# The first batch of an attention-and-FFN kernel: other fills, mask products that open banks, conversions and a raw load in other places

## The chip, the cores and the metric

The kernel runs on one core of a Trainium2 chip. The metric is the time of one execution in device microseconds (us); the median of the runs shown is taken. PE is the matrix engine (PEld its weight loads), DVE, ACT and POOL are the vector, scalar and general engines, SP issues most DMAs.

## The reference

Eight batches of 576 tokens go through attention with eight heads of 64, and the result (4608 tokens of 512) through a two-layer FFN with a gate:

```python
scores = scale * np.matmul(q, k.transpose(0, 1, 3, 2))
mask_local = (rel >= 0) & (rel < stride)
mask_strided = (rel >= 0) & (pos[None, :] % stride == pos[:, None] % stride)
...
attn = np.exp(scores)
attn = attn / (np.sum(attn, axis=-1, keepdims=True) + 1e-09)
return np.matmul(attn, v).astype(np.float32)
...
h = x @ w_in
g = np.where(pos, h, np.where(neg, 0.0, (h + beta) ** 2 / (4.0 * beta)))
return (g @ w_out).astype(np.float32)
```

The weights come as 64-bit floats, held as pairs of 32-bit words.

## The kernel before

**Attention** of a batch is cut into four units: units 0 and 1 are the local heads, units 2 and 3 the strided ones. The masks leave few keys for each query, so a unit is a set of small score products. For unit u the steps have letters, and a string of them (`AGENDA`) gives the order by hand: `s` scores on PE (`qk` of the batch, two pairs of heads), `o` a product of zeros that opens the score banks, `i` the mask added in the bank by a product with the identity (`m_loc`, `m_str`, made by POOL), `g` a plain copy out of PSUM on ACT, `m` copy with mask on DVE, `X`/`x` row maxima on DVE, `S`/`a`/`b` maxima subtracted, `e` exponentials on ACT, `q` row sums on DVE, `p` plus epsilon on ACT, `w`/`r` normalising (a reciprocal on DVE, then a product on DVE for `w`, on POOL for `r`), `f` transposes on PE (`tp`), `c`/`d` copies of them on ACT or DVE (`pT`), `v` the values product on PE (`xp`), `h`/`l` the high and low part of the result (`xq_a` on ACT, `xq_b` on DVE) for the first 512 tokens left to `H`/`M` where the digits ask for the other part. `Z` issues fills: products of zeros into banks that a later step uses, whose result nobody reads.

**Weights** are converted on the chip, block by block (f = 0 to 15, i = 0 for `w_in`, 1 for `w_out`): a raw load of 512 KB (`load_w`, SP queue), then the steps `A`, `L` (ACT), `B` (DVE), `C` (POOL), `D` (ACT, high part; `g` the same on DVE), `E` (DVE, low part). Step `E0.0` finishes block 0 of `w_in`, and so on. While the FFN of the first 512 tokens runs, these conversions stand between its steps.

**The FFN's start.** `up(0, f)` is 12 products of 128x512 into one bank (high times high, high times low, low times high, over four blocks `cc` of channels, of which 0 and 1 are local heads and 2 and 3 strided ones). Blocks f = 0 and 1 are split: `U0`, `V0` are the first 4 products each (high weights, `cc` 0 and 1), `U1`, `V1` the other 8. After them come `1F0`, `1F1` (loads of batch 1's values), `1s0` (scores of batch 1) and `W7` (raw loads of block 7), then `up(0, 2)`, `down(0)`, `1s1`, `up(0, 3)` and so on. `gate(f)` is two passes on ACT and one on DVE, `rounded(f)` two on DVE; `down(f)` waits for them.

**What sets the order.** Each engine runs its instructions in the order in which the code records them, which is the agenda's; a line of the agenda begins with the time at which it is due against the FFN's steps (minus 66.69: all of it ahead of the FFN). The loads of SP are recorded ahead of the agenda: `qk` of batch 0 (four loads), the raw load of block 0, values and raw loads in turn. The first raw load is held back by a copy of one element into its buffer (L447) that reads `qk` 1, so that the load waits for that copy.

Of the kernel before, what the change touches and what calls it, by code (L numbers as in the profile page):

```python
# [1382 lines left out]
```

## Time and profile before

| what | value |
|---|---|
| median of 3 runs | 802.41 us (801.7 to 802.97) |
| the profiled execution's own time | 803.35 us |
| its span in the trace | 801.2 us |
| PE, DVE, ACT, POOL busy | 99%, 77%, 63%, 32% of the span |

The span is what the trace shows from the first instruction to the last; 2.15 us of the profiled execution lie around it. PE's busy time counts every matmul, those of zeros too, and the ends of matmuls are modelled, so 99% doesn't say that the work is at PE's peak; it says that little of the span has no matmul on PE.

### The profile page before, as it was taken

Reading aid. Unit: us, or ns where it says so; the run is one execution under the profiler, and the core shown is the slowest. Engines: PE = TensorE matmul, PEld = TensorE weight load, DVE = VectorE, ACT = ScalarE, POOL = GpSimd, SP = SyncE. Lnnn points to the kernel's source line nnn. Section 1 sums busy time; section 2 is a strip of 40 time slices with the busy share of each in tenths; the row PEclk is TensorE's granted clock in tenths of the full one; section 3 lists DMA queues with packets and bytes.
Section 4 is the critical chain, followed back from the end, with each engine's and each line's share of the span. In section 5 each row is a group of like instructions: output and inputs, shape, how many; then the busy total and the mean of one; then the engine's idle time right before and its main releaser. Section 6 shows DMA issues by size and latency. Waiting matters only on the chain.

```text
span 801.2 us, 17214 instructions
## 1 busy us (share of the span) xinstructions
PE 791.7 (99%) x6641; PEld 646.5 (81%) x6641; DVE 618.7 (77%) x855; ACT 503.6 (63%) x854; POOL 259.6 (32%) x202
## 2 busy tenths in 40 slices
PE   8999999999999999999999999999999999999998
PEld 5778888878888888878888888888888888888886
DVE  4899979898989999978679786675786854566673
ACT  4899764566764555677665455778544667775442
POOL 4466325897674320022141102132424001224000
PEclk9999999999999999999999999999999999999999
DMA  9967878998899999898789778777787676666765
GB/s 345 390 218 250 334 259 291 300 295 301 268 335 315 293 304 349 271 292 272 240 255 305 232 224 262 240 230 225 214 263 238 210 243 195 190 195 188 221 199 167
DMA packets 106224, 208.67 MB, mean 260 GB/s; under 512 B 17696, under 2 KB 30496, under 8 KB 104096
## 3 DMA queue, kind: packets, MB, share of 16 engines
q1 hardware_dynamic: 99088, 178.09, 69.3%
q10 hardware_dynamic: 7056, 29.49, 9.9%
q8 instruction: 53, 0.87, 0.5%
q14 instruction: 27, 0.22, 0.1%
HBM read 160.76 MB, written 46.78 MB: 259 GB/s over the span
## 4 chain that ended last, share of the span: by engine, by line
PE 87%; DVE 4%; DMA 4%; issue 1%; SPq 1%; POOL 1%; ACT 1%; ACTq 0%; DVEq 0%; POOLq 0%
PE yo L1188 22%; PE y L1093 16%; PE zo L1188 11%; PE h L940 9%; PE z L1093 8%; PE xo L1188 5%; PE o L1000 5%; PE x L1093 4%; PE sc L617 3%; PE xp L832 2%; DMA qk<-in_qk_s 1%; DMA v_w<-in_v_w 1%; DMA windows<-t 1%; PE xp L820 1%; DVE st L524 1%
## 5 line engine op out<-in xcount | busy, mean ns | idle before, releaser
L1188 PE MATMUL yo<-hl,wr 128*128 128x512 f32 x768 | 177.6, 390 | 0.0
L1188 PEld LDWEIGHTS yo<-hl,wr 128*128 128x128 f32 x768 | 143.6, 188 | 30.8 <-DVE hl L1050 0.9
L1093 PE MATMUL y<-x,wr 128*128 128x512 f32 x576 | 139.9, 390 | 0.0
L1093 PEld LDWEIGHTS y<-x,wr 128*128 128x128 f32 x576 | 108.0, 188 | 22.5
L940 PE MATMUL h<-xq_a,w 128*128 128x512 f32 x384 | 123.3, 395 | 0.0
L1149 POOL TENSOR_TENSOR ga<-gb,ga 128x1024 f32<-128x1024 f32 x17 | 44.1, 2602 | 235.3 <-DVE ga L950 175.6
L1050 DVE TENSOR_TENSOR hl<-ga,hl 128x1024 fp32r<-128x1024 f32 x48 | 64.1, 1351 | 35.9 <-ACT hl L1049 35.8
L1188 PE MATMUL zo<-hl,wr 128*128 128x512 f32 x384 | 89.3, 391 | 0.0
L940 PEld LDWEIGHTS h<-xq_a,w 128*128 128x128 f32 x384 | 72.0, 188 | 16.3 <-DVE g L950 0.4
L1188 PEld LDWEIGHTS zo<-hl,wr 128*128 128x128 f32 x384 | 71.6, 188 | 15.6 <-DVE hl L1050 0.6
L1049 ACT CAST hl<-ga 128x1024 fp32r<-128x1024 f32 x48 | 49.9, 1050 | 50.9 <-PE yo L1188 16.5
L1093 PE MATMUL z<-x,wr 128*128 128x512 f32 x288 | 73.6, 391 | 0.3 <-DVE ga L1075 0.3
L940 PE MATMUL h<-xq_b,w 128*128 128x512 f32 x192 | 73.6, 391 | 0.1
L1093 PEld LDWEIGHTS z<-x,wr 128*128 128x128 f32 x288 | 53.7, 188 | 12.0 <-DVE ga L1075 0.8
L947 ACT ACTIVATE tmp<-tmp 128x512 f32<-128x512 f32 x96 | 60.8, 633 | 3.1
L1050 DVE TENSOR_TENSOR hl<-gb,hl 128x1024 fp32r<-128x1024 f32 x36 | 49.2, 1379 | 13.8 <-ACT hl L1049 13.7
L516 POOL TENSOR_TENSOR st<-st 128x256 f32<-128x256 f32 x48 | 52.8, 1102 | 15.0 <-DVE st L733 6.2
L1049 ACT CAST hl<-gb 128x1024 fp32r<-128x1024 f32 x36 | 37.7, 1056 | 31.3 <-PE zo L1188 15.3
L950 DVE SCALAR_TENSOR_TENSOR ga<-ga,tmp 128x512 f32<-128x512 f32 x48 | 33.0, 688 | 28.3 <-ACT tmp L947 28.1
L944 ACT ACTIVATE u<-h,half 128x512 f32<-128x512 f32 x48 | 32.9, 686 | 30.1 <-PE h L940 22.5
L481 POOL TENSOR_TENSOR raw<-raw 128x512 uint32<-128x512 uint32 (+1 forms) x33 | 35.4, 1082 | 43.1 <-DVE raw L477 15.5
L710 POOL TENSOR_TENSOR pr<-pr,st 128x384 f32<-128x384 f32 (+3 forms) x18 | 25.7, 1432 | 64.2 <-DVE st L706 64.0
(128 smaller groups left out, 1404.0 us busy)
## 6 DMA issues: line engine op xcount, KB each, us to landing
wr<-ks SPq DMA_DIRECT2D x224, 256.0 KB, 3.9
wr<-kq SPq DMA_DIRECT2D x168, 256.0 KB, 3.4
ks<-st ACTq DMA_DIRECT2D x16, 1024.0 KB, 5.7
raw<-in_w SPq DMA_DIRECT2D x31, 512.0 KB, 7.6
qk<-in_qk_s SPq DMA_DIRECT2D x16, 604.0 KB, 6.5
qk<-in_qk_l SPq DMA_DIRECT2D x16, 576.0 KB, 6.5
kq<-w ACTq DMA_DIRECT2D x16, 512.0 KB, 4.1
out<-kept SPq DMA_DIRECT2D x24, 256.0 KB, 3.8
```

Of the source, the lines that this page charges most:

```text
L481: nc.gpsimd.tensor_tensor(out=raw[:, :, 1], in0=raw[:, :, 1], in1=raw[:, :, 0], op=ALU.add)
L516: eng.tensor_tensor(out=st[:, to, 1], in0=st[:, x, 1], in1=st[:, y, 1], op=op)
L940: nc.tensor.matmul(o_ps[c, f], weight(f, 0, h)[:, x, e:e + P], xq[c][y][:, cc], start=first and n == 0, stop=last and n == len(todo) - 1)
L944: nc.scalar.activation(u, h, AF.Relu, bias=half, scale=0.5)
L947: nc.scalar.activation(u, u, AF.Square)
L950: nc.vector.scalar_tensor_tensor(out=to, in0=h, scalar=1.0, in1=u, op0=ALU.max, op1=ALU.min)
L1000: nc.tensor.matmul(o_ps["o"][d], weight(f, 1, h)[:, x, e:e + P], gs[y], start=f == 0 and n == 0, stop=f == NF - 1 and n == 2)
L1049: nc.scalar.copy(t[:, 0], src)
L1050: nc.vector.tensor_tensor(out=t[:, 1], in0=src, in1=t[:, 0].bitcast(F32), op=ALU.subtract)
L1093: nc.tensor.matmul(to, w_[:, a, c * P:(c + 1) * P], xc[m][:, b, c], start=m in (1, 2, 5) and c + q == 0, stop=c == 1 and q == 2, skip_grou ...
L1149: eng.tensor_tensor(out=to, in0=x, in1=y, op=op)
L1188: nc.tensor.matmul(to, w_[jj][:, a, d * P:(d + 1) * P], t[:, b, jj], start=m in (1, 2, 5) and k + jj + q == 0, stop=k == NP // 2 - 1 and j ...
```

## The change

- **Fills.** The zeros tile becomes a float32 tile (`nothing`), of which `zeros` is a bfloat16 view. `Z` takes a number of products and a letter: without `b` they are float32 (128x384 here), with `b` bfloat16 over the whole bank. Ahead of unit 0's scores stand 2 + 2 of them instead of 17; 1 + 3 + 2 before unit 0's transposes instead of 3 + 14; 2 before the values products of units 0 and 1 each; those before units 2 and 3 are gone.
- **Masks.** For units 1 and 3 the step `I` (new) puts the mask's product first, as the one that opens the bank and closes it; the scores add to it. `o` and `i` of these units are gone (4 products of zeros fewer).
- **First conversion.** `A0.0` stands behind `0e1` on ACT instead of ahead of it.
- **First raw load.** The copy that holds it back reads one element of `m_str` (partition 64) instead of `qk` 1. The raw load of block 2 moves ahead of the values of unit 3.
- **The end of the first batch.** The values of unit 2 come before those of unit 3. `U0`, now 6 products (with low weights), stands between them; `V0`, 6, behind unit 3; then `U1` (4), `U2` (2), `V1`, `V2`. On DVE `E0.0` moves ahead of the low parts of units 2 and 3. `H1`, `M1`, `H2`, `M2` move behind `gate(0)`, which is now in the agenda as `H0`. The steps `A0.1` to `E0.1` are spread forward.
- **Banks.** The transposes and values of the first batch use other banks; from block 4 of the second token chunk on, `up` turns over four banks instead of three.

```diff
--66.69 0Zs0:17 0o0 0s0 0o1 0i0 0X0 0s1 0i1 0S0 0o3 0g1 0x1 0s2 0Zv0:3 0Zf0:3 0m2 0e0 0a1 A0.0 0s3 0i3 0e1 0x2 0q0
--66.69 0p0 0g3 0a2 0q1 0Zf0:9 0e2 0w0 0Zf0:5 0f0 0p1 0x3 0c0 B0.0 0v0 0b3 L0.0 0e3 0r1 0q2 0p2 0f1 C0.0 0r2 0q3
--66.69 A1.0 0d1 D0.0 0p3 0h0 0r3 L1.0 0l0 A2.0 0Zf2:4 0v1 B1.0 0f2 0h1 0d2 0f3 0c3 0Zv3:4 0v3 0l1 0H1 L2.0 C1.0 g1.0 0v2 E1.0
--66.69 0M1 0h3 B2.0 0l3 E0.0 0h2 0H3 C2.0 U0 0l2 g2.0 V0 0M3 U1 0H2 0M2 E2.0 V1 1F0 1F1 A3.0 1s0 A0.1 B3.0 W7
--66.69 B0.1 L0.1
--63.035 A3.1 C0.1 A4.0 A1.1
--59.845 L3.0 C3.0 B1.1 D0.1 L1.1 C1.1 1m0 E0.1 1x0 1a0
+-66.69 0Zs0:2 0Zs0:2b 0o0 0s0 0I1 0i0 0X0 0s1 0S0 0I3 0g1 0x1 0s2 0Zf0:1 0m2 0e0 0a1 0s3 0e1 A0.0 0x2 0q0
+-66.69 0p0 0g3 0a2 0q1 0e2 0w0 0Zf0:3 0Zf0:2b 0f0 0Zv0:2b 0p1 0x3 0c0 B0.0 0v0 0b3 L0.0 0e3 0r1 0q2 0p2 0f1 0Zv1:2b C0.0 0r2 0q3
+-66.69 A1.0 0d1 D0.0 0p3 0h0 0r3 L1.0 0l0 0v1 B1.0 0f2 0h1 A2.0 0d2 0f3 0c3 C1.0 0v2 0l1 g1.0 E0.0 B2.0 0h2
+-66.69 0l2 L2.0 C2.0 A0.1 U0 0v3 0h3 L0.1 E1.0 B0.1 C0.1 0l3 V0 0H3 0M3 g2.0 E2.0 U1 A3.0 U2 V1 V2 B3.0 H0 D0.1 0H1 0M1 E0.1 0H2 0M2 1F0 1F1 1s0 W7
+-63.035 A1.1 A3.1 A4.0
+-59.845 L3.0 C3.0 B1.1 L1.1 C1.1 1m0 1x0 1a0
...
-    zeros = const.tile([P, P], BF16, name="zeros")
-    nc.vector.memset(zeros, 0.0)
+    nothing = const.tile([P, P], F32, name="nothing")
+    nc.vector.memset(nothing, 0.0)
+    zeros = nothing.bitcast(BF16)[:, :P]
...
-            nc.scalar.copy(raws[f][0:1, i, 0:1, 0].bitcast(F32), after)
+            nc.scalar.copy(raws[f][64:65, i, 0:1, 0].bitcast(F32), after)
...
-            N = min(t.shape[1], 256)
+            of = zeros if short_ else nothing
             for _ in range(n):
-                nc.tensor.matmul(t[:, :N], zeros, zeros[:, :1].broadcast_to([P, N]), start=True, stop=True)
+                nc.tensor.matmul(t, of, of[:, :1].broadcast_to(list(t.shape)), start=True, stop=True)
...
+        def masked(u):
+
+            local, b0, _ = UNITS[u]
+            ahead[u, "s"] = ts = banks(u, "s")
+            covered.add(u)
+            done_.add(u)
+            n, W = slots(u)[0], WL if local else WS
+            m = m_loc[:, b0 and 1:][:, :n].unsqueeze(2) if local else m_str.unsqueeze(1).unsqueeze(1)
+            for t in ts:
+                nc.tensor.matmul(t, ident_b, m.broadcast_to([P, n, 2, W]), start=True, stop=True)
...
-            tag = ("b2", "b3") if NF * c + f < NF + 4 else ("b2", "b3", "b0")
+            tag = ("b2", "b3") if NF * c + f < NF + 4 else ("b0", "b1", "b2", "b3")
...
+            kinds_ = (((0, 0), (0, 1), (1, 0)), ((0, 0), (1, 0)), ((0, 1),))[part]
+            todo = [(cc, x, y) for x, y in kinds_ for cc in ((2, 3) if part else (0, 1))]
...
-        load_w(0, 0, loaded[0, 1, "qk"][0:1, 0, 0:1])
+        load_w(0, 0, m_str[64:65, 0:1])
         load_v(0, 0)
         load_v(0, 1)
         load_w(1, 0)
         load_v(0, 2)
+        load_w(2, 0)
         load_v(0, 3)
-        load_w(2, 0)
```

The built programs show the moves. On ACT, from the exponentials of unit 0 on (`pr_0`; `raw` 191 is block 0 of `w_in`, `st_0` unit 0's statistics), before:

```order
L717 ACTIVATE pr_0_297<-pr_0_297 128x768
L469 ACTIVATE raw_191<-raw_191 128x512
L717 ACTIVATE pr_1_333<-pr_1_333 128x384
L725 ACTIVATE st_0_298<-st_0_298 128x12
L676 COPY pr_3_410<-sc_3_0_329 128x4x54
```

and after:

```order
L729 ACTIVATE pr_0_284<-pr_0_284 128x768
L729 ACTIVATE pr_1_318<-pr_1_318 128x384
L470 ACTIVATE raw_191<-raw_191 128x512
L737 ACTIVATE st_0_285<-st_0_285 128x12
L688 COPY pr_3_386<-sc_3_0_314 128x4x54
```

The conversion and unit 1's exponentials have changed places; the small step of unit 0 still stands behind the conversion. On DVE, at the low parts of the last units (`xq_b`) and the low part of the weights (`w_0`; raw 191 is block 0, raw 198 block 1), before:

```order
L903 TENSOR_TENSOR xq_b<-xp_3_0_581,xq_a 128x12x16
L903 TENSOR_TENSOR xq_b<-xp_3_0_581,xq_a 128x2x16
L903 TENSOR_TENSOR xq_b<-xp_3_1_582,xq_a 128x12x16
L903 TENSOR_TENSOR xq_b<-xp_3_1_582,xq_a 128x2x16
L494 TENSOR_TENSOR w_0_516<-raw_191,w_0_516 128x2x256
L903 TENSOR_TENSOR xq_b<-xp_2_0_614,xq_a 128x18x16
L903 TENSOR_TENSOR xq_b<-xp_2_1_615,xq_a 128x18x16
```

and after:

```order
L491 CAST w_0_491<-raw_198 128x2x256
L495 TENSOR_TENSOR w_0_491<-raw_191,w_0_491 128x2x256
L478 TENSOR_SCALAR raw_202<-raw_202 128x512
L915 TENSOR_TENSOR xq_b<-xp_2_0_551,xq_a 128x18x16
L915 TENSOR_TENSOR xq_b<-xp_2_1_552,xq_a 128x18x16
L495 TENSOR_TENSOR w_0_491<-raw_198,w_0_491 128x2x256
L478 TENSOR_SCALAR raw_191<-raw_191 128x512
L915 TENSOR_TENSOR xq_b<-xp_3_0_596,xq_a 128x12x16
```

Block 0's low weights (from raw 191) now come ahead of the low parts of units 2 and 3. On PE, at the last values products and the first products of the FFN, before:

```order
L832 MATMUL xp_2_0_614<-pT_2_568,v_2_None 64x64 x2
L832 MATMUL xp_2_1_615<-pT_2_568,v_2_None 64x64 x2
L940 MATMUL h_0_660<-xq_a,w_0_516 128x512 x2
L940 MATMUL h_0_660<-xq_b,w_0_516 128x512 x2
L940 MATMUL h_1_669<-xq_a,w_0_516 128x512 x2
```

and after:

```order
L844 MATMUL xp_2_0_551<-pT_2_537,v_2_None 64x64 x2
L844 MATMUL xp_2_1_552<-pT_2_537,v_2_None 64x64 x2
L953 MATMUL h_0_589<-xq_a,w_0_491 128x512 x2
L953 MATMUL h_0_589<-xq_b,w_0_491 128x512 x2
L953 MATMUL h_0_589<-xq_a,w_0_491 128x512 x2
L844 MATMUL xp_3_0_596<-pT_3_547,v_3_204 64x64 x2
```

Six products of the FFN's block 0 now stand ahead of unit 3's values, low weights among them.

## Rows read from the trace of the kernel before

**Rows 1.** Stretches: length, busy us (instructions) by engine, PEclk, DMA share, GB/s
```profile
0.00:10.20 10.20, 9.11 (x223) 6.36 (x224) 3.07 (x8) 3.16 (x7) 5.84 (x26) 1.00 0.82 293
10.20:12.55 2.35, 0.00 (x0) 0.00 (x0) 2.06 (x3) 0.20 (x1) 1.61 (x3) 1.00 0.97 356
12.60:16.00 3.40, 3.39 (x49) 2.39 (x49) 1.65 (x3) 1.82 (x7) 0.19 (x1) 0.50 1.03 416
12.55:24.80 12.25, 11.73 (x254) 9.43 (x253) 9.05 (x22) 9.89 (x28) 5.43 (x6) 0.86 1.03 410
25.40:34.00 8.60, 8.46 (x185) 6.48 (x185) 6.66 (x21) 6.83 (x20) 2.08 (x2) 1.00 1.02 407
34.00:100.00 66.00, 65.94 (x550) 53.47 (x551) 63.56 (x119) 60.84 (x112) 36.57 (x34) 1.00 0.77 275
```

**Rows 2.** Timeline of PE: start, length, line, operation, count, [idle before, releaser]
```profile
0.99 3.81 PE L599 MATMUL sc<-zeros 128*128 128x256 bf16 x17 [0.99 <-DVE zeros L379]
...
5.37 1.32 PE L617 MATMUL sc<-qk 64*32 64x64 f32 x96
...
12.61 0.58 PE L599 MATMUL tp<-zeros 128*128 128x256 bf16 x2 [2.51 <-issue]
...
15.11 2.15 PE L599 MATMUL tp<-zeros 128*128 128x256 bf16 x14
17.10 0.82 PE L747 MATMUL tp<-ident,pr 128*128 128x128 f32 x6
...
22.05 1.42 PE L747 MATMUL tp<-ident,pr 128*128 128x128 f32 x11
...
25.44 0.46 PE L832 MATMUL xp<-pT,v 54*64 54x64 f32 x16 [0.78 <-issue]
...
26.53 0.73 PE L940 MATMUL h<-xq_a,w 128*128 128x512 f32 x2
```

**Rows 3.** DMA queue of instructions in 10.2 to 11.3, and 16.0 to 17.3: packets, MB
```profile
q8 instruction: 1, 0.02, 5.1%
...
q8 instruction: 1, 0.02, 4.8%
```

**Rows 4.** Timeline of ACT, columns as for PE
```profile
5.79 0.19 ACT L447 COPY raw<-qk 1x1 f32<-1x1 f32 x1 [3.76 <-DMA qk<-in_qk_l]
...
12.35 0.66 ACT L469 ACTIVATE raw<-raw 128x512 f32<-128x512 f32 x1 [2.31 <-DMA raw<-in_w]
...
13.32 0.20 ACT L725 ACTIVATE st<-st 128x12 f32<-128x12 f32 x1
15.09 1.00 ACT L676 COPY pr<-sc 128x216 f32<-128x216 f32 x4 [1.57 <-PE sc L641]
...
17.63 0.86 ACT L757 COPY pT<-tp 128x384 f32<-128x384 f32 x2 [0.67 <-PE tp L747]
```

**Rows 5.** Timeline of DVE, columns as for PE
```profile
14.17 0.96 DVE L734 TENSOR_TENSOR pr<-pr,st 128x768 f32<-128x768 f32 x1
...
27.62 0.70 DVE L494 TENSOR_TENSOR w<-raw,w 128x512 fp32r<-128x512 f32 x1
28.23 1.31 DVE L903 TENSOR_TENSOR xq_b<-xp,xq_a 128x288 fp32r<-128x288 f32 x2
...
39.52 0.68 DVE L494 TENSOR_TENSOR w<-raw,w 128x512 fp32r<-128x512 f32 x1
```

**Rows 6.** Timelines of POOL (second half of the strided mask) and SP (first raw load)
```profile
6.02 0.54 POOL L398 TENSOR_SCALAR_AFFINE_SELECT m_str<-m_str 64x54 bf16<-64x54 bf16 x2
...
6.00 0.33 SPq L448 DMA_DIRECT2D raw<-in_w  x1
```

**Rows 7.** Line 537, loads of `qk`, to 20 us: first and last issue; issue to landing
```profile
L537 SPq DMA_DIRECT2D qk<-in_qk_l x4: 327/360/417, 0.7 to 18.1; - x4
...
DMA to landing us min/median/max: 3.5/6.3/10.9
```

**Rows 8.** Chain of waits, one piece: start, length, what (the products of `up(0, 2)`)
```profile
33.97 2.96 PE h L940 x12
```

More of the change, by code (lines that the diff above doesn't have):

```diff
@@ L490, in conv_d, with conv_e @@
             copy(to[:, :, 0], whole(raw))
-    def conv_e(f, i):
+    def conv_e(f, i, eng=nc.vector):
         for raw, to in words(f, i):
-            nc.vector.tensor_tensor(out=to[:, :, 1], in0=whole(raw), in1=to[:, :, 0].bitcast(F32), op=ALU.subtract)
+            eng.tensor_tensor(out=to[:, :, 1], in0=whole(raw), in1=to[:, :, 0].bitcast(F32), op=ALU.subtract)
     def blocks(i, j):
@@ L575, in wide @@
             return b > 1 and u == 0
-        probs, flipped, there, ahead, covered = {}, {}, {}, {}, set()
+        probs, flipped, there, ahead, covered, done_ = {}, {}, {}, {}, set(), set()
         def banks(u, kind):
@@ L618, in score @@
                                          qk[:, k0:k0 + W], start=u not in covered,
-                                         stop=u not in covered)
+                                         stop=u not in covered or u in done_, skip_group_check=u in done_)
         def score_0(u):
@@ L909, in in_two @@
             return lambda u: do(u, rest if b == 0 else None)
[L911 removed]
+        steps = {"s": score, "y": score_0, "z": score_1, "m": mask, "o": opened, "I": masked, "i": cover, "g": plain, "X": most_there, "S": below_there, "x": most, "w": norm_v, "a": below_max, "e": expo, "q": total, "p": plus_eps, "k": plus_eps_v, "b": below_max_v, "r": norm,
                  "f": flip, "t": turn, "j": spread, "J": gather, "c": keep, "d": keep_v, "v": value, "V": values_1_3, "h": in_two(high, False), "l": in_two(low, False), "H": in_two(high, True), "M": in_two(low, True),
@@ L916, in go @@
                 if name[0] == "Z":
-                    zero(int(name[2]), name[1], int(name[4:]))
+                    zero(int(name[2]), name[1], int(name[4]), name[5:] == "b")
                     continue
@@ L924, in tile_sparse_attention_then_ffn, with up @@
     o_ps, outs = {}, {}
-    def up(c, f, first=True, last=True):
+    def up(c, f, part=None):
+        first, last = part in (None, 0), part in (None, 2)
         if first:
-            tag = ("b2", "b3") if NF * c + f < NF + 4 else ("b2", "b3", "b0")
+            tag = ("b2", "b3") if NF * c + f < NF + 4 else ("b0", "b1", "b2", "b3")
             o_ps[c, f] = bank(tag[(NF * c + f) % len(tag)], [P, CH], f"h_{c}_{f}")
@@ L933, in up @@
             todo.sort(key=lambda n: n[2])
-        if not (first and last):
-            todo = [(cc, 0, y) for y in range(2) for cc in ((0, 1) if first else (2, 3))]
-            todo += [] if first else [(cc, 1, 0) for cc in range(NC)]
+        if part is not None:
+            kinds_ = (((0, 0), (0, 1), (1, 0)), ((0, 0), (1, 0)), ((0, 1),))[part]
+            todo = [(cc, x, y) for x, y in kinds_ for cc in ((2, 3) if part else (0, 1))]
         for n, (cc, x, y) in enumerate(todo):
@@ L1193, in down_block @@
             between(n)
-    FREE = {"s0": "oo", "s1": "aa", "s2": "hh", "s3": "oo", "f0": "oo", "f1": "hh", "f2": "oo", "f3": "oo",
-            "v0": "aa", "v1": "hh", "v2": "oo", "v3": "aa"}
-    first = attention(0, lambda u, kind: FREE[kind + str(u)][0])
+    B01, B45 = ("b0", "b1"), ("b4", "b5")
+    FREE = {"s0": "o", "s1": "a", "s2": "h", "s3": "o", "f0": B01, "f1": "h", "f2": B01, "f3": "h",
+            "v0": "a", "v1": B45, "v2": B01, "v3": "a"}
+    first = attention(0, lambda u, kind: FREE[kind + str(u)])
     MORE = set("2s2 2v0 2v1 3s0 3s2 3v1 4s0 4s1 4v0 5s0 5s2 5v1 5v2 6s3 7s0 7s1 7v0 7v1".split())
@@ L1254, in step @@
                 x_step(*map(int, rest.split(".")))
+            elif name == "H0":
+                gate(0)
             elif kind in "UV":
-                up(0, int(kind == "V"), rest == "0", rest == "1")
+                up(0, int(kind == "V"), int(rest))
             elif kind == "Z":
@@ L1294, in tile_sparse_attention_then_ffn @@
                 up(0, f)
-            todo = [(GATE, lambda: gate(f)), (ROUNDED, lambda: pend.append((f, rounded(f))))]
+            todo = [(GATE, lambda: gate(f))] if f else []
+            todo += [(ROUNDED, lambda: pend.append((f, rounded(f))))]
             if f > 1:
```

10 lines of the change are left out of this document (5 added, 5 removed).

## Prediction

> **What bounds the kernel now.** I read the busy time by stretch first [rows 1]. From 34 to 100 us PE is busy for 65.94 of 66.00 us, and the page's busy share of 99% says that it goes on like that: behind the first batch, the time is PE's row of products, which the change leaves as it is. So what counts is when that row begins. `up(0, 2)`, the first whole block, starts at 33.97 [rows 8]; ahead of it lie the first batch's attention and the split blocks 0 and 1, whose products start at 26.53 [rows 2]. A change there is worth the microseconds by which 33.97 comes earlier, as long as ACT and DVE keep up behind it.
>
> In the first 34 us I read PE's timeline next [rows 2]. It stops twice, for 2.51 us until 12.61 and for 0.78 us until 25.44, and both times the releaser is "issue": it waits for nothing that the trace shows. The counts say what it is [rows 1]: 223 matmuls and 224 weight loads, 447 instructions, run before the first stop, and 254 and 253, 507, between the two. One packet of the queue of instructions moves in 10.2 to 11.3, another in 16.0 to 17.3 [rows 3], while the data queues fill the DMA engines (share 0.97 and more [rows 1]). I read this as PE running out of instructions, which come in pieces of about 254, two of them at hand, and whose loads queue behind data. After the first stop the granted clock is 0.50 from 12.6 to 16.0 [rows 1], 1.2 GHz instead of 2.4: PE had stood for 2.5 us.
>
> The Trainium skill (Runtime: NRT & Kernel Launch, Instruction fetch mechanics) also has the stream refilled in blocks of 256 instructions, but calls the cost of crossing a block "mostly hidden". The rows show 2.51 and 0.78 us that nothing hides. By the page's rule the first stop would have another cause and stay where it is; that is the first rival below.
>
> **Part by part.**
>
> *Fills and masks at the start.* The 17 fills took 3.81 us from 0.99 on [rows 2], at half the clock. They only cover the wait for `qk`: the second pair of scores can't start before `qk` 1 has landed, at 5.79 [rows 4]. A float32 fill of 384 columns has no row. Eleven float32 transposes of 128 columns take 1.42 us [rows 2], 0.13 each, and a float32 product runs as two records (48 in the program are the x96 at 5.37); that makes 2 x 3 x 0.13 = 0.77 us at most at the full clock. Below it stands what a bfloat16 fill of that width takes, 2.15 / 14 x 1.5 = 0.23, partly at half clock. I take 0.7, since the transposes are float32 too. Two of them at half clock and four bfloat16 products of 0.34 (3.81 / 17 x 1.5) end at 0.99 + 2.8 + 1.4 = 5.2, ahead of 5.79: cost 0, up to 0.6 if the first pair of scores then ends late. The products of zeros that `I` saves (4) lie in the same waits: 0.
>
> *The first stop.* After the change unit 2's scores end at the 412th instruction (12 in fills, 4 to open, 192 + 8 + 96 + 4 + 96), a fill makes 416, and the 447th is 31 into unit 3's 80. PE gets there at about 10.10 + 0.4 = 10.5, instead of stopping at 10.10. Whether it stops depends on when the next piece arrives. No row shows when PE asks. If it asks when the older piece is used up, that is the 193rd instruction, 155 of 192 into unit 0's scores: 5.37 + 1.32 x 155/192 = 6.4. By then SP has issued the first raw load (6.00 [rows 6]), and the packet moves only after 10.2 [rows 3]. After the change the raw load waits for the mask: POOL ends it at 6.02 + 0.54 = 6.56 [rows 6], the copy takes 0.19 [rows 4], so 6.8, while PE asks at about 6.5. Then the packet has only `qk` 2 and 3 ahead of it. So the stop costs between 0 (the piece is there) and 2.1 us (it comes as late as now). I take 0, since the request passes the raw load by 0.3 us, and keep 2.1 for the range. With the stop goes the half clock: 3.40 us at half speed is up to 1.7 us.
>
> *The raw load 0.8 us later*, with every load behind it on SP. ACT waits 2.31 us for it, until 12.35 [rows 4], and unit 0's chain hangs on that. The engines are full without a break, so the load's place in the line, not its issue, sets its landing: 0; if the delay went through whole, 13.15.
>
> *A0.0 behind unit 1's exponentials.* Unit 0's small step `p0` then starts at 12.35 + 0.66 = 13.0 instead of 13.32 [rows 4], and on DVE unit 1's row sum no longer stands between (it is done by 13). The normalising product of unit 0, now at 14.17 [rows 5], can start at 13.0 + 0.2 + 0.2 = 13.4: 0.8 earlier, done at 14.35. If the raw load lands 0.8 later, nothing.
>
> *Unit 0's transposes* start at 17.10 [rows 2], long after that product: PE is late through the stop, the half clock and 14 fills (2.15). After: 10.5, the rest of unit 3's scores 0.4, three float32 fills and two others 2.5, makes 13.4, under the 14.35: they start at 14.4, 2.7 earlier. On ACT the copy of unit 3's scores (1.00, now waiting for PE until 15.09 [rows 4]) runs at 13.2, then 0.8 of exponentials and a small step, so the copy of unit 0's transposes, now at 17.63 [rows 4], starts at 15.0: 2.6 earlier. If the first stop stays, transposes start at 16.9, 0.2 earlier.
>
> *To the end of the batch.* DVE and ACT do the same work as before. Of the 20.85 us in the two stretches of 12.55 to 34, ACT is idle for 4.1 and DVE for 5.1 [rows 1]: that is what can be squeezed out. DVE's row sums and copies, which wait for ACT at each turn, pass on 2.0 of the 2.6. The second stop (0.78) falls away: the 959th instruction is now in unit 3's values, behind U0, and the piece was asked for earlier. U0 with six products ahead of unit 3 fills 6 x 2.96/12 = 1.5 us [rows 8] in which PE waited; what it needs, `E0.0`, ran at 27.62, behind unit 3's low parts, with 1.31 for unit 2 after it [rows 5], and now runs first. I count 1.3. Together 2.0 + 0.8 + 1.3 = 4.1: `up(0, 2)` at 29.9. Ahead of it stand the scores of batch 1, whose second load was issued at 18.1 and landed 10.9 later [rows 7], 29.0; half of the scores (0.6) after that makes 29.6, so it doesn't bind, but no more than 4.4 can be had.
>
> *Behind it.* PE runs ahead of DVE and ACT then. `E3.0` on DVE, for `up(0, 3)`, ends at 39.52 + 0.68 = 40.20 [rows 5], and PE has no slack around it (65.94 of 66.00). DVE and ACT come earlier only by the idle time that they lose: of 4.1 and 5.1 about 0.9 and 1.8 stay (waits for unit 2's and 3's products), so 3.2 to 3.3. I take 3.2. The bank turn over four and `H1` to `M2` behind gate 0 get 0: PE's idle time there is 0.06 us, and these parts are read in the second chunk only.
>
> Sum: 803.35 - 3.2 = 800.15 for an execution like the profiled one; the median is 0.94 below that one, so **799.2**. About 0.2% (1.6 us) is what a measurement can tell from no change.
>
> **Rivals.** *The first stop stays* (PE asks later than I think, the queue takes the packet no earlier, or the page's rule holds). For it: the second packet too moved 3.4 us or more after PE went on at 12.55 [rows 1, 3], behind data. The transposes gain 0.2, the end of the batch its 0.8 + 1.3: 2.1 to 2.3 earlier, 800.2. *DVE and ACT give it back*: they are busy for 96% and 92% from 34 to 100 [rows 1], and if their first batch is not squeezed, PE waits at `E3.0` and its like; only the 0.8 of unit 0 is left, 801.6. Against it: 4 to 5 us of idle time ahead of 34. *Slower: the clock.* The change leaves few fills between 13.4 and 24, where PE will wait for ACT and DVE often, and a stop of 2.5 us was followed by half clock. If the clock falls there and stays low, the transposes and values of four units and the first products, about 6 us at 2.4 GHz, take 12: 6 - 3.2 = 2.8 later, 805.2. It decides the sign once more than 3.2 us of PE's work on the path run at half clock. Against it: no single wait that I work out is over 1.4 us.
>
> **How the numbers follow.** Forecast 0.60 (2.4 to 4.4 earlier: 798.0 to 800.0), stop stays 0.17 (799.9 to 801.0), given back 0.16 (800.9 to 803), clock 0.05, the rest 0.02 on either side. The range 797.8 to 801.6 leaves out half of "given back", the clock case and the tails, 0.16. Faster by over 0.2%: 0.60 + 0.14 = 0.74; within 0.2%: 0.03 + 0.16 = 0.19; slower 0.07.
>
> **What would show it.** In the changed kernel's trace: no "issue" stop near 10.5 and a packet of instructions that starts at about 8.5 to 9.5; granted clock 1.00 from 12.6 to 16; ACT's first conversion still at 12.3; unit 0's transposes at 14.4; the scores of batch 1 at 29 and `up(0, 2)` at 29.6 to 30; PE waits of under 1 us in all between 34 and 100. A stop of 2 us at 10.5, a raw load that lands at 13, or a clock of 0.50 after 16 would make the prediction wrong, each in the step named.

## The result: slower by half a per cent

| | before | changed |
|---|---|---|
| median of 22 runs each | 802.44 us (800.88 to 806.92) | 806.29 us (802.42 to 812.33) |
| ratio, 95% interval | | 1.0052 (1.0037 to 1.0067) |
| profiled execution, its span | 803.35, 801.2 us | 811.82, 809.6 us |

The forecast was 799.2 (797.8 to 801.6), faster. The mean granted clock tells two kinds of runs of the changed kernel apart: 11 of its 22 have 0.999 or more and a median of 804.8 us, 7 have 0.996 or less and a median of 811.1, and 4 lie between. Of 129 runs of the kernel before that were taken beside the experiments, 4 have 0.996 or less; the 110 with 0.999 or more have a median of 802.0. So there are two losses to explain: some 2.8 us at the full clock, and 6 us more in a third of the runs.

The profile after is of the second kind. PE's timeline (start, length, line, operation, count, [idle before, releaser]), beside [rows 2]:

```profile
11.44 2.54 PE L600 MATMUL tp<-nothing 128*128 128x384 f32 x8
14.27 0.85 PE L759 MATMUL tp<-ident,pr 128*128 128x128 f32 x6 [0.29 <-DVE pr L746]
...
15.38 1.84 PE L844 MATMUL xp<-pT,v 64*64 64x32 f32 x86
20.09 0.63 PE L844 MATMUL xp<-pT,v 64*64 64x32 f32 x10 [2.88 <-issue]
...
21.85 1.69 PE L844 MATMUL xp<-pT,v_None 64*64 64x32 f32 x48
...
27.15 0.74 PE L953 MATMUL h<-xq_a,w 128*128 128x512 f32 x2
```

The stop at the 447th instruction is gone, as forecast. In its place PE stops for 2.88 us inside unit 0's values, ten records before their end, and again the releaser is "issue". Stretches beside [rows 1] (length, busy us and instructions by engine, PEclk, DMA share, GB/s) let its records be counted up to that stop:

```profile
0.00:10.80 10.80, 9.63 (x223) 5.52 (x225) 3.45 (x8) 3.20 (x8) 6.36 (x27) 1.00 0.83 291
10.80:17.20 6.40, 6.04 (x142) 4.18 (x134) 5.92 (x13) 5.54 (x15) 2.62 (x4) 1.00 1.01 400
...
20.10:26.60 6.50, 6.50 (x94) 5.62 (x98) 4.30 (x12) 3.24 (x8) 2.13 (x2) 0.50 1.03 407
26.70:35.10 8.40, 8.40 (x195) 6.34 (x188) 7.32 (x20) 7.00 (x22) 2.08 (x2) 1.00 1.02 407
```

Matmuls and weight loads counted together, 448 and 276 less the 24 that were under way at 10.80 and stand in both lines, PE stops ahead of its 701st record; the two stops of [rows 2] stand ahead of the 448th and the 955th. These are steps of about 254 records, and I read what lies between two of them as one piece of instructions. The queue of instructions moves its second packet at 17.64, where the kernel before moves it at 16.16 (in the second window of [rows 3]); PE goes on 2.45 us behind it. From the end of the stop on the granted clock is 0.50 for 6.83 us (19.84 to 26.67), where the kernel before had 3.41: unit 1's 48 values take 1.69 us instead of 1.09.

ACT and DVE beside [rows 4, 5], up to the stop:

```profile
11.68 0.68 ACT L470 ACTIVATE raw<-raw 128x512 f32<-128x512 f32 x1 [0.40 <-DMA raw<-in_w]
12.81 0.97 ACT L688 COPY pr<-sc 128x216 f32<-128x216 f32 x4
14.83 0.86 ACT L769 COPY pT<-tp 128x384 f32<-128x384 f32 x2 [0.18 <-PE tp L759]
```

```profile
13.17 0.96 DVE L746 TENSOR_TENSOR pr<-pr,st 128x768 f32<-128x768 f32 x1
```

Up to here the forecast's times hold: transposes at 14.27 (forecast 14.4), their copy at 14.83 (15.0), the normalising product at 13.17 (13.4), the raw load issued at 6.79 (6.8). Only the first conversion, at 11.68, comes earlier than the forecast 12.3.

### The profile page after: what moved, and what is told of

It is laid out like the page before. It is cut to its first block, busy times and chain, and to the rows that moved or that the text cites. A ratio compares the mean times of both kernels' runs of the same rounds, so it can differ in the third digit from the quotient of the medians.

```text
span 809.6 us, 17160 instructions
## 1 busy us (share of the span) xinstructions
PE 794.1 (98%) x6612; PEld 645.3 (80%) x6612; DVE 617.4 (76%) x855; ACT 504.8 (62%) x854; POOL 258.8 (32%) x202
## 4 chain that ended last, share of the span: by engine, by line
PE 82%; DVE 6%; DMA 4%; POOL 2%; ACT 2%; SPq 1%; issue 1%; DVEq 0%; POOLq 0%
PE yo L1201 22%; PE y L1106 15%; PE zo L1201 11%; PE h L953 9%; PE z L1106 8%; PE xo L1201 5%; PE x L1106 4%; PE o L1013 3%; PE xp L844 2%; DMA qk<-in_qk_s 2%; PE sc L618 2%; DMA wr<-ks 1%; POOL st L517 1%; DMA windows<-t 1%; PE tp L759 1%
## 5 line engine op out<-in xcount | busy, mean ns | idle before, releaser
L953 PEld LDWEIGHTS h<-xq_a,w 128*128 128x128 f32 x384 | 71.7, 188 | 17.3 <-DVE w L495 1.5
L1062 ACT CAST hl<-gb 128x1024 fp32r<-128x1024 f32 x36 | 37.7, 1056 | 31.3 <-PE zo L1201 15.3
```

Of the source, the lines that this page charges most:

```text
L953: nc.tensor.matmul(o_ps[c, f], weight(f, 0, h)[:, x, e:e + P], xq[c][y][:, cc], start=first and n == 0, stop=last and n == len(todo) - 1)
L1062: nc.scalar.copy(t[:, 0], src)
```

## The experiments

In all of them "third piece" is the second packet of the queue of instructions, the next one after PE has passed the 448th record. The expectations count 449 and 705, and the prediction 959, where the records put the stops ahead of the 448th, the 701st and the 955th. Each time in that column is from one trace of the kernel. The last columns count the runs whose mean clock is 0.996 or less, and give the median of those at 0.999 or more.

| kernel | ratio (95% interval) | third piece at, stop ahead of the 701st (us) | runs at 0.996 or less | median at 0.999 or more |
|---|---|---|---|---|
| changed | 1.0052 (1.0037 to 1.0067) | 17.64, 2.88 | 7 of 22 | 804.8 |
| a_qktie | 1.0021 (1.0001 to 1.0040) | 17.83, 3.20 | 2 of 12 | 804.4 |
| b_masktie | 1.0000 (0.9988 to 1.0012) | 14.33, none | 0 of 12 | 802.4 |
| a_hold | 1.0071 (1.0047 to 1.0095) | 12.32, none | 6 of 12 | 805.4 |
| b_4banks | 0.9994 (0.9983 to 1.0004) | 14.42, none | 0 of 12 | 801.9 |
| a_oldtail | 1.0049 (1.0022 to 1.0076) | 17.59, 2.92 | 5 of 12 | 803.8 |
| a_oldfront | 1.0021 (1.0006 to 1.0036) | 14.46, none | 0 of 12 | 803.5 |
| a_fills | 1.0020 (1.0003 to 1.0037) | 14.93, 0.43 | 1 of 12 | 803.7 |
| a_shift | 1.0038 (1.0019 to 1.0057) | 14.43, none | 0 of 7 | 805.7 |
| b_newfills | 1.0009 (0.9995 to 1.0023) | 14.40, none | 0 of 12 | 802.4 |
| a_shift8 | 1.0086 (1.0056 to 1.0115) | 17.93, 3.30 | 6 of 8 | 803.2 (one run) |
| a_noI | 1.0030 (1.0011 to 1.0049) | 14.72, none | 0 of 9 | 803.8 |
| a_A00 | 1.0085 (1.0060 to 1.0110) | 18.24, 3.20 | 3 of 6 | 807.9 (two runs) |
| c_d11 | 1.0025 (1.0010 to 1.0041) | 14.83, none | 1 of 12 | 803.4 |
| a_d11 | 1.0063 (1.0039 to 1.0088) | 17.84, 3.20 | 5 of 11 | 804.2 |
| c_best | 1.0017 (1.0001 to 1.0032) | 15.92, 0.65 | 0 of 12 | 802.1 |
| h_best | 1.0073 (1.0045 to 1.0100) | 12.26, none | 4 of 10 | 806.5 |

**The raw load's tie, undone and alone; the four banks alone.**

```diff
-        load_w(0, 0, m_str[64:65, 0:1])
+        load_w(0, 0, loaded[0, 1, "qk"][64:65, 0, 0:1])
```

is a_qktie; b_masktie is the same line the other way round in the kernel before. b_4banks changes only the turn of `up` there.

> The changed kernel with one part undone: the copy that holds the first raw load reads qk 1 again, so that the load goes out at about 6.0 instead of 6.8 us. The instruction order of every engine is that of the changed kernel. Theory A (instructions): the time is set by when PE's pieces of 256 instructions arrive, each asked for when PE passes into a new one and each queued behind the data that SP has asked for by then. The second piece then moves at about 10 instead of 8.4, PE stops near 10.8 for 1.5 to 2.3 us with half clock behind it, and the stop of 2.9 us at the 705th instruction shrinks to under 1, since PE comes there later. up(0, 2) starts at 33 to 35 us; time 803 to 807, ratio to the kernel before 1.000 to 1.006. Theory B (order): the loss comes from the new order (DVE, ACT, banks) and not from where PE stops; then the tie is worth nothing and the time stays at 806 (1.005), stop or no stop.

> The kernel before with one part of the change alone: the copy that holds the first raw load reads the strided mask, so that the load goes out at 6.8. Theory A: the second piece of instructions moves at about 8.4 to 9, the stop of 2.5 us at the 449th instruction falls away, the third piece, asked for at about 10.2 with all of SP's loads ahead of it, moves at 16 to 17.6, and PE stops at the 705th instruction for 1 to 3 us instead, with half clock behind it; time within 3 us of before, 801 to 805 (0.998 to 1.004). Theory B: with the stop gone the front is 0.5 to 2 us earlier and nothing takes its place: 800 to 802 (0.997 to 0.999).

> The kernel before with one part of the change alone: from block 4 of the second token chunk on, the products turn over four banks instead of three. Theory A: no effect, 802.4 (0.999 to 1.001). Theory C (the later waits of the changed kernel, near 168, 191 and 234 us, come from the banks): new waits of 1 us and more between 130 and 250 us, 804 to 807 (1.002 to 1.006).

Alone the tie is worth nothing: b_masktie has 1.0000, and with the raw load issued at 6.28 (a_qktie) the first packet still moves at 8.48. In the changed kernel undoing it gives 1.0021 instead of 1.0052; at the full clock the two medians are 804.4 and 804.8, and whether 2 low clocks in 12 runs are fewer than 7 in 22 so few runs don't say. The four banks alone change nothing (0.9994), as theory A of b_4banks had it. More telling is its first batch, which is the kernel before, unchanged. Its packet moves at 8.42, not at the 10.25 of [rows 3], and PE doesn't stand at the 448th record, between the fills and unit 3's scores (PE's timeline):

```profile
9.98 0.51 PE L599 MATMUL xp<-zeros 128*128 128x256 bf16 x3
10.32 0.74 PE L599 MATMUL tp<-zeros 128*128 128x256 bf16 x3
10.99 0.92 PE L617 MATMUL sc<-qk 64*64 64x54 f32 x40
...
15.07 0.84 PE L747 MATMUL tp<-ident,pr 128*128 128x128 f32 x6 [1.23 <-DVE pr L734]
16.16 2.94 PE L832 MATMUL xp<-pT,v 64*64 64x32 f32 x96 [0.24 <-ACT pT L757]
...
32.28 0.50 PE L940 MATMUL h<-xq_a,w 128*128 128x512 f32 x1
```

So the 2.51 us of [rows 2], on which most of my gain rested, belonged to that execution. In 18 of the 19 other traces of this study this packet moves at 8.0 to 8.8; the one where it moves at 9.70 (c_best) has a stop of 1.57, and two others stop for 0.53 and 0.73 us (a_fills, c_d11). Both theories that I had written for the tie fall: no stop took the place of the first one in b_masktie, and nothing was won. The last line shown is `up(0, 2)`, at 32.28 instead of 33.90. The values at 16.16 take 2.94 us instead of the 1.98 of the kernel before: the granted clock is 0.50 for 3.41 us from 16.85 on, though PE had waited for DVE (1.23 us) and not for instructions.

**The loads held back.** a_hold issues the loads behind unit 0's values only when unit 1's exponentials are done.

```diff
-0e0 0a1 0s3 0e1 A0.0
+0e0 0a1 0s3 0e1 T A0.0
...
+        def later_loads():
+            raws[1] = place(PLACES[1], [P, 2, DM, 2], U32, "raw_1")
+            nc.scalar.copy(raws[1][64:65, 0, 0:1, 0].bitcast(F32), held[0][64:65, 0, 0:1])
...
```

> The changed kernel with the loads behind the values of unit 0 (raw load of block 1 first, then the rest) held back until unit 1's exponentials are done (about 11.3 us), by a copy of one element on ACT ahead of A0.0, so that the third piece of instructions, asked for at about 10.8, has only the raw load of block 0 and the values of unit 0 ahead of it. Theory A: that piece moves at 12.5 to 14.5 instead of 17.6, the stop of 2.9 us at the 705th instruction is under 0.5, the granted clock doesn't fall there (or a later piece stops PE for under 2 us), up(0, 2) starts at 30.5 to 33 and the time is 799 to 803 (0.996 to 1.001). Theory B: the loads are 1 to 2 us later, nothing is won, and the time is 806 or more (1.005 or more).

In its trace the third piece moves 1.6 us after PE passed the 448th record, instead of 6.8 in the profile after, and the stop is gone (PE's timeline):

```profile
15.29 1.96 PE L846 MATMUL xp<-pT,v 64*64 64x32 f32 x96
...
22.05 0.74 PE L955 MATMUL h<-xq_a,w 128*128 128x512 f32 x2
```

With fewer loads outstanding, then, the piece comes sooner than in any other kernel here (3.3 us and more, below; h_best, which holds the loads back too, has 1.6 again). The time is another matter: 1.0071. Theory A had the mechanism and missed the time, which is theory B's. The scores of batch 1 then wait for their load (0.43 us), and half of the runs still have a low clock; no trace of such a run of this kernel was taken, so what happens in them is open.

**The start and the end of the batch apart, and the old number of fills.** a_oldtail has the changed start (fills, masks, `A0.0`, tie) with the old rest (but the changed banks of the first batch); a_oldfront the old start with the changed rest; a_fills is the changed kernel with 17, 6, 14, 4 and 4 fills of 256 bfloat16 columns in the old places.

> The changed kernel's first two agenda lines (fills, mask products, A0.0, tie of the raw load) with the rest as in the kernel before (units 3 and 2, U and V in their old cut, conversions, order of raw load 2 and the values of unit 3, three banks). Theory D (two causes): runs with a mean granted clock of 0.999 or more lose by the end of the batch and the conversions, runs at 0.996 or less by the front with few fills. Then the full-clock runs fall from 804.8 to 801.5 to 803, a quarter or more of the runs still has 0.996 or less, and the median is 802 to 805. Theory E (the front alone): full-clock runs stay at 804 to 805, median 804.5 to 807.

> The other half: first two agenda lines as in the kernel before (17 + 6 + 14 fills of 256 bfloat16 columns, old mask products, A0.0 ahead of unit 1's exponentials, raw load tied to qk 1), the rest as changed. Theory D: at most 1 run of 12 has a mean clock of 0.996 or less, the full-clock runs are at 803.5 to 805.5 and so is the median (1.002 to 1.004). Theory E: 801.5 to 803 (0.999 to 1.001).

> The changed kernel with the number of fills of the kernel before (17 ahead of unit 0's scores, 6 and 14 before its transposes, 4 ahead of unit 2's transposes, 4 before unit 3's values, of 256 bfloat16 columns). Theory F (the clock falls because PE has too little to do between 10 and 20 us): the runs at 0.996 or less vanish (at most 1 of 12), median 803.5 to 805.5. Theory A (a stop for instructions, whatever is filled, takes the clock): a third of the runs still has 0.996 or less, median 805.5 to 808.

The low clock goes with the start (5 of 12 with it, 0 of 12 without), and both halves cost at the full clock: 1.8 us with the changed start (7 runs), 1.5 with the changed rest (6 runs), on the 802.0 of before. Theory D had the rest alone for that. With more fills the late piece is gone in a_fills, as theory F had it (1 of 12, median 803.8), but they add instructions as well as time.

**The changed kernel again, as it is.**

> The changed kernel as it is, a second look. Theory A: if the mean clock is 0.999 or more, the stop at the 705th instruction is under 2 us and up(0, 2) starts at 31 to 33 us; if it is 0.996 or less, the stop is 2.5 us or more and half clock lasts over 5 us behind it. In both, 1 us or more is lost between 40 and 62 us against the kernel before.

> The changed kernel as it is, a third look. With a mean clock of 0.999 or more: third piece at 14 to 15.5, stop in unit 0's values under 1 us, up(0, 2) at 31 to 33, then 1.4 us or more lost between 40 and 60 us. With 0.996 or less: third piece at 17 to 18, as in the two looks before.

a_again is the profile after once more (809.24 us, third piece at 17.82, stop 2.92). a_again2 is a run at the full clock (805.88 us, third piece at 14.82). PE's timeline of a_again2:

```profile
14.51 0.85 PE L759 MATMUL tp<-ident,pr 128*128 128x128 f32 x6 [0.32 <-DVE pr L746]
...
15.61 1.96 PE L844 MATMUL xp<-pT,v 64*64 64x32 f32 x96
...
22.37 0.73 PE L953 MATMUL h<-xq_a,w 128*128 128x512 f32 x2
...
30.39 0.50 PE L953 MATMUL h<-xq_a,w 128*128 128x512 f32 x1
...
43.49 0.73 PE L953 MATMUL h<-xq_a,w 128*128 128x512 f32 x2 [0.46 <-DVE w L495]
...
56.01 0.57 PE L618 MATMUL sc<-qk 64*64 64x54 f32 x24 [1.06 <-DMA qk<-in_qk_s]
57.38 0.57 PE L618 MATMUL sc<-qk 64*64 64x54 f32 x24 [0.80 <-DMA qk<-in_qk_s]
```

With the piece there in time, PE's first batch goes close to the forecast, and `up(0, 2)` starts at 30.39 (forecast 29.9). Yet this run is slower than the median of before by 3.4 us. I put the products of the FFN of each trace beside those of b_masktie, whose time is that of before (802.78 us in its trace); the table gives how much later the same product starts, in us:

| kernel | `U0` | `up(0, 2)` | `up(0, 4)`, first | its fifth | last of `down(3)` | `up(0, 6)`, behind `1s2` | last |
|---|---|---|---|---|---|---|---|
| b_masktie, its own start | 23.98 | 31.30 | 43.72 | 44.63 | 55.07 | 56.23 | 796.65 |
| before | 2.55 | 2.60 | 2.38 | 2.39 | 2.38 | 2.67 | 0.58 |
| after | 3.17 | 3.89 | 3.47 | 4.20 | 4.31 | 5.92 | 8.92 |
| a_again2 | -1.61 | -0.91 | -1.30 | -0.56 | -0.50 | 1.65 | 2.97 |
| a_oldfront | -0.69 | -0.01 | -0.41 | 0.30 | 0.42 | 1.08 | -0.15 |
| a_oldtail | 4.39 | 4.41 | 4.23 | 4.23 | 4.23 | 4.23 | 4.07 |
| c_d11 | 0.43 | 2.32 | 2.69 | 2.69 | 2.69 | 2.76 | 2.09 |
| a_d11 | 3.14 | 3.90 | 4.28 | 4.29 | 4.29 | 5.01 | 5.01 |

The changed end of the batch loses 0.7 us inside `up(0, 4)`, which waits for `E4.0`, and 0.7 to 2.2 us at `1s2`, the strided scores of batch 1. The old end loses at most 0.3 there, early or late (before, a_oldtail). Between a_again2 and the profile after, a full clock and a low one, lie 4.8 us at `up(0, 2)` and 6.0 at the last product. From 60 us on single executions drift apart: before makes up 2.1 us on b_masktie, while the profile after, which waits 1.77 us for DVE at 191 us (`xq_b`) and 1.43 for "issue" at 234, loses 3.0 more. Whether such waits come with the change I can't tell; a_oldtail and a_d11 have no such drift.

Who is late at 57 us is told by the chain of waits of a_again2 (start, length, what; it doesn't touch PE from 25 us on until the scores):

```profile
34.43 0.82 ACT w L491 x2
35.45 1.26 ACT raw L474 x2
36.71 0.56 ACT raw L470
37.30 0.77 DVE raw L478 x2
38.11 0.86 POOL raw L482
39.15 1.57 POOL raw L482
40.72 0.36 POOL empty L427
41.10 0.68 SPq L431
...
44.96 0.58 SPq L432
45.59 0.42 SPq L449
...
47.73 0.45 SPq L538
48.27 9.06 DMA qk<-in_qk_s
57.38 0.57 PE sc L618 x24
```

Conversions on ACT and DVE, POOL's empty tile, SP's window writes and raw loads queued behind it, and at last the load of `qk`, 9.06 us from issue to landing. An earlier first batch doesn't make this chain earlier. In b_masktie the same load is issued at 46.19 instead of 47.73, and the chain lies on PE from 41.32 on.

**Which part makes the third piece late.** a_shift adds 21 fills of 16 columns (42 instructions, next to no time), a_shift8 four of them, b_newfills has the new fills alone in the kernel before, a_noI the old mask products in the changed kernel, a_A00 `A0.0` in its old place. Their edits to the agenda, in this order:

```diff
-0Zs0:2 0Zs0:2b
+0Zs0:9n 0Zs0:2n 0Zs0:2 0Zs0:2b
...
-0Zs0:2 0Zs0:2b
+0Zs0:4n 0Zs0:2 0Zs0:2b
...
-0Zs0:9s 0Zs0:8s
+0Zs0:2 0Zs0:2b
...
-0I1 0i0 0X0 0s1 0S0 0I3
+0o1 0i0 0X0 0s1 0i1 0S0 0o3
...
-0s3 0e1 A0.0
+A0.0 0s3 0e1
```

> The changed kernel with 21 fills of 16 bfloat16 columns more (11 ahead of unit 0's scores, 4 ahead of unit 3's, 6 ahead of unit 0's transposes): 42 instructions with next to no time in them, so that the steps of 256 instructions fall on the same places of the program as in the run with the old number of fills (a_fills), while PE is filled no longer than in the changed kernel. Theory S (where the step falls decides): the third piece moves at 14 to 15.5, the stop in unit 0's values is under 1 us, at most 2 of 12 runs have a mean clock of 0.996 or less, median 803 to 805. Theory F (the time that PE is filled decides): the third piece moves at about 17.6, the stop is 2.5 us or more, a third of the runs has 0.996 or less, median 805.5 to 808.

> The kernel before with the changed fills alone (2 + 2, 1, 3 + 2 and the two pairs before values, float32 and bfloat16; none ahead of units 2 and 3). Theories S and F: the third piece comes late (17 us or more) in a good part of the runs, PE stops 2 us and more in unit 0's values, a quarter or more of the runs has a mean clock of 0.996 or less (1 of 64 in the kernel before), the others stay near 802 to 803, median 802.5 to 806. Theory G (the slow runs need the moved A0.0 or the mask products, not the fills): at most 1 of 12 at 0.996 or less, median 801.5 to 802.5.

> The changed kernel with 4 fills of 16 bfloat16 columns more ahead of unit 0's scores: 8 instructions, as many as the four products of zeros that the mask products saved. Theory S8 (the place of the step of 256 decides, and 8 instructions are enough, since the kernel before with the new fills alone, which has these 8, has no slow runs): third piece at 14 to 15, stop in unit 0's values under 1 us, at most 1 of 12 runs at 0.996 or less, median 803.5 to 805. Theory S40 (it takes more, or it is A0.0's place): third piece at 17 to 18, stop of 2.5 us or more, a third of the runs at 0.996 or less, median 805.5 to 808.

> The changed kernel with the masks of units 1 and 3 as before (products of zeros that open the banks, masks added behind the scores; 4 products more). Theory M: at most 2 of 12 runs at 0.996 or less, third piece at 14 to 15.5, median 803.5 to 805. Theory A0: a third or more at 0.996 or less, median 805.5 to 809.

> The changed kernel with A0.0 ahead of unit 1's exponentials again. Theory A0 (its place makes unit 0's transposes early, and so PE reaches the step before the piece is there): transposes at 14.8 to 15.5, at most 2 of 12 runs at 0.996 or less, median 803.5 to 805. Theory M (the mask products): a third or more of the runs stays at 0.996 or less, median 805.5 to 809.

Theory S holds against F in the piece and the clock (a_shift: 14.43, no low clock in 7 runs), though its median, 805.7, lies outside the range of S; 8 instructions don't do it (a_shift8: 17.93, 6 of 8). The fills alone do no harm (b_newfills: G). `A0.0` isn't it (a_A00: 18.24, 3 of 6); with the old mask products the late piece is gone (a_noI: 14.72, 0 of 9).

One trace for each kernel proves little here, since the changed kernel itself has the piece early in a_again2 and late in the two other traces. The clock of the runs carries it. All seven traces with a mean clock of 0.996 or less have the late piece, none of the 13 others. Of the kernels with the new mask products and the small number of fills, the loads not held back, 28 of 71 runs have such a clock (changed, a_qktie, a_oldtail, a_shift8, a_A00, a_d11); of the nine that lack one of the two, 2 of 100. So the late piece comes with the new mask products and the small number of fills together. Why, stays open. PE passes the 448th record at 10.4 to 11.2 in all of these, and up to 15.1 us SP's loads are issued much alike, yet the queue takes the piece 3.3 to 4.0 us later in the one case and 6.8 to 7.4 in the other. SP's next raw load is issued at 15.9 to 16.2 in the late traces and at 16.7 to 17.5 in most of the early ones (16.1 in c_d11); which of the two is the cause, no run tells. Nor is the loss then cured: where the third piece comes in time, a later step is waited for. PE's timeline of a_shift, and of a_noI:

```profile
23.23 0.50 PE L845 MATMUL xp<-pT,v_None 54*64 54x64 f32 x17 [1.29 <-issue]
```

```profile
23.61 0.21 PE L844 MATMUL xp<-pT,v_None 54*64 54x64 f32 x1 [1.26 <-issue]
```

Both have half clock for 3.41 us behind it.

**One conversion put back.** The change also moves `D1.1` (ACT) ahead of `L5.0`, and `E1.1` (DVE) forward with it; neither the list of its parts nor the forecast names this move. c_d11 is a_oldfront, and a_d11 the changed kernel, with `D1.1` and `E1.1` where they were; c_best has besides that batch 1's loads of `qk` ahead of the raw loads of block 3; h_best puts both into a_hold.

```diff
--55.845 D3.0 E3.0 D1.1 L5.0 L2.1 A5.0 B5.0 C5.0 B4.0
--55 E1.1
--54.19 L4.0 C4.0
+-55.845 D3.0 E3.0 L5.0 L2.1 A5.0 B5.0 C5.0 B4.0
+-54.19 L4.0 C4.0 D1.1 E1.1
```

> a_oldfront (old fills, masks, tie and A0.0; changed end of the batch, conversions and banks) with one conversion back where it was: D1.1 (ACT) and E1.1 (DVE) behind L4.0 and C4.0. Theory H (D1.1 ahead of L5.0 on ACT makes the gates, POOL's conversions, E4.0 and the loads of qk behind POOL late): the losses between 43 and 57 us (0.7 and 0.7 us against the kernel with the old order) fall under 0.3 each, the full-clock runs go from 803.5 to 802 to 802.8. Theory I (the low parts, E0.0 beside POOL's conversion and the later H and M parts on DVE make it late): they stay at 0.5 or more each, 803 to 804.5.

> The changed kernel with D1.1 and E1.1 back behind L4.0 and C4.0. Theory H: the losses at the products that wait for E4.0 and at the scores 1s2 go (together under 0.5 us instead of 1.4 to 3), the full-clock runs are at 802.5 to 804 instead of 804.8, the slow ones stay: a third at 0.996 or less at 808 to 810; median 803.5 to 806. Theory I: losses and times as in the changed kernel.

> c_d11 with the two loads of qk of batch 1 (local heads) ahead of the two raw loads of block 3. Theory Q (in a run without a stop the scores of batch 1 wait for their load, which takes away what U0 ahead of unit 3 gains): the scores start 0.5 to 1 us earlier than in c_d11, at 29.2 to 29.8, and the time is 0.3 to 1 us less, 801 to 802.5. If the scores aren't held by the load, or block 3 is late then, the time is that of c_d11 or more.

> a_hold (loads behind the values of unit 0 held back) with D1.1 and E1.1 back and the loads of qk of batch 1 ahead of the raw loads of block 3. If what was seen adds up: against a_hold 1.2 to 1.7 us less behind the batch and up to 1 us at the scores of batch 1; full-clock runs at 802 to 803.5 instead of 805.4; half of the runs still with half clock, 806 to 809. If the earlier front is given back elsewhere, the full-clock runs stay above 804.

The wait for `E4.0` goes in both (0.00 and 0.01 instead of 0.7, table above), that at `1s2` in c_d11 (0.07) and in part in a_d11 (0.72). `D1.1` is the second conversion in the chain's first line above. But c_d11 now waits at `down(1)`, for `E1.1`:

```profile
44.00 0.73 PE L1013 MATMUL o<-gh,w 128*128 128x512 f32 x2 [0.45 <-DVE w L494]
```

and the times don't follow: 803.73 (1.0025, 1.0010 to 1.0041) beside 1.0021 for a_oldfront, and 807.86 (1.0063, 1.0039 to 1.0088) for a_d11, 5 of whose 11 runs have a low clock (its four runs at the full clock have 804.2, beside 804.8). Theory H names the place of the two waits, then, and not the loss: what PE no longer waits for `E4.0` it mostly waits for `E1.1`. c_best gives 803.38 (1.0017, 1.0001 to 1.0032); stops for instructions of 1.57 and 0.65 us in its trace hide what the earlier loads do. Its 5 runs at the full clock have 802.1, within theory Q's range, beside 803.4 of the 4 of c_d11, too few to call Q shown. h_best gives 807.81 (1.0073, 1.0045 to 1.0100): in its trace the scores of batch 1 no longer wait for their load, and PE waits 1.96 us for the first gate on DVE instead. No version beat the kernel before. What at the full clock the changed start costs (1.8 us in a_oldtail) has no such wait in a trace and stays open, and so does the 1.5 of a_oldfront, which c_d11 keeps without the two waits.

## Why the prediction was wrong

- **The start from one execution.** Step "the first stop": the packet at 8.5 to 9.5 and no stop at 10.5 came true (8.40), for a reason that wasn't the change's: the kernel before has them too where its first batch stands unchanged (b_4banks). I set the profiled execution's 2.51 us of stop and 3.4 us of half clock into the sum, as the 2.0 of its 4.1, and took that execution's whole distance to the median as 0.94. Without that stop unit 0's transposes start at 14.47 and 15.07 in the old order (b_masktie, b_4banks), so the change's 14.27 and 14.51 (a_again2) are 0 to 0.8 earlier and not 2.7; `up(0, 2)` starts at 31.3 and 32.3, not at 33.9, and against this the 30.39 of a_again2 is 0.9 to 1.9 earlier, not 4.1. That the stop itself costs little is in the traces too: b_masktie starts `up(0, 2)` 2.6 us earlier than before and ends 0.6 us earlier.
- **"The second stop (0.78) falls away … the piece was asked for earlier."** In a_again2 and the profile after no stop stands there (in b_4banks neither), but the step failed one piece earlier: I followed the last request of the batch and not the one between. PE has the 700 records before that step behind it at 17.2, and in the profile after the piece moves only at 17.64. Being early isn't enough for the stop: b_masktie is at the same step at 16.82 and a_again2 at 17.19, both with the piece there. What the sum had no term for is a piece that moves 6.8 us after the step before and not 3.3 to 4.0; why it does so stays open. That there was no slack could have been worked out from [rows 1, 3] and the expected order: from 10.8 on PE goes through a piece in 6.4 us, and with loads outstanding a piece is there some 5.5 to 6.6 us after the step before (3.3 to 4.0, and 2.2 to 2.6 until PE goes on; an estimate from the traces here). The Trainium skill (Runtime: NRT & Kernel Launch, Instruction fetch mechanics) calls the crossing mostly hidden; in [rows 2] and in the trace after the measurement is 0.78 to 2.9 us that nothing hides.
- **The clock rival**, at 0.05, had the clock right and the reason wrong. It let the clock fall because few fills are left and PE waits for ACT and DVE; in the profile after it fell at the stop for instructions, which wasn't among the waits "that I work out", and a_shift, filled no longer, has no such run in 7. Its price, 805.2, is near the median by luck: the median mixes runs at the full clock, 804.8, with runs at 811.1.
- **"Behind it" 3.2 of 4.1 stay, waits of under 1 us up to 100 us.** Wrong at the full clock too: in a_again2 0.74 us inside `up(0, 4)` and 2.15 at `1s2`. The second rival had waits of this kind ("`E3.0` and its like") and a loss of the gain, but no loss beyond it. I took the bound to be DVE's and ACT's busy share, and didn't follow the load of `qk` back through SP to POOL and ACT. The move of `D1.1`, which sits in that chain, has no term in the sum.
- **E0.0 ahead of the low parts** took what I gave it, 0.68 us beside the 0.70 of [rows 5]. What I missed is `E1.0`, which now stands behind unit 2's low part and beside POOL's conversion of block 2: 1.45 us in a_again, where the kernel before had 0.69. DVE's timeline of the kernel before, and of a_again (`E0.0`, then `E1.0`), and POOL's of a_again:

```profile
24.44 0.69 DVE L494 TENSOR_TENSOR w<-raw,w 128x512 fp32r<-128x512 f32 x1
```

```profile
26.36 0.68 DVE L495 TENSOR_TENSOR w<-raw,w 128x512 fp32r<-128x512 f32 x1
...
28.98 1.45 DVE L495 TENSOR_TENSOR w<-raw,w 128x512 fp32r<-128x512 f32 x1
```

```profile
28.84 1.04 POOL L482 TENSOR_TENSOR raw<-raw 128x512 uint32<-128x512 uint32 x1 [3.99 <-ACT raw L474]
```

  The Trainium skill (SBUF — State Buffer, SBUF: two separate sides) says that a DVE instruction with two inputs from SBUF and a POOL instruction that reads SBUF take turns at one port pair, for a whole instruction each; the trace agrees: from POOL's end at 29.88 the pass takes 0.55 more. How much of this 0.76 us reaches the time, no run shows.
- **Right:** the fills (float32, 0.64 us each where I took 0.7), the raw load at 6.8, transposes and their copy to 0.2 us, and `up(0, 2)` to 0.5 us in the one trace where no piece is late. As these times were forecast as gains over the profiled execution, that they came true says little for the gain. One reading of the start isn't in the rows: "at half the clock" for the 17 fills rests on their length alone (0.22 us each, where the three at 9.48 start 0.11 apart), since [rows 1] print 1.00 for that stretch.

## What to carry to other kernels

Before a gain is built on a stop in a profile, see whether the stop is in a second execution with the same instructions up to there; here it wasn't. Where an engine runs small instructions, count them up to each step and ask when the next piece can be there, for the changed order as well as the old one. And follow the next late load back through its queue: an engine that becomes free earlier only helps if that chain gets earlier with it.

## What the runs showed of the hardware

- In the first 30 us PE's stops for instructions of 0.4 us and more stand ahead of the 448th, the 701st or 702nd and the 952nd to 955th record, in every kernel here that has one. With SP's loads outstanding the second and third packet mostly move 3.2 to 4.1 us after the step (the second 6.8 to 7.4 in seven traces, all of them with the few fills and the new mask products); with the loads held back it was 1.6. PE goes on 2.2 to 2.6 us behind the packet's start.
- The granted clock fell to 0.50 for 6.83 us at the stops of 2.9 to 3.3 us (seven traces), and for 3.41 us behind the 2.51 of the kernel before and behind stops of 1.17 to 1.37 before `U0` (a_fills, a_shift, a_noI, c_d11). Behind stops of 0.56 and 0.62 at the same place it stayed at 1.00 (a_oldfront, b_masktie). Waits for another engine go with it as well: 3.41 us at 0.50 follow a wait of 1.23 us for DVE in b_4banks, and one of 1.96 us for DVE in h_best.
- A DVE product of two float32 inputs (128x512) took 1.45 us where a POOL instruction of 1.04 us had begun 0.14 us before it, and 0.68 us without one (a_again).
